# Clustered attention and two mixers on one core: a list scheduler for the order of attention, similarities in two row groups

## The chip, the cores and the metric

The kernel runs on one core of a Trainium2 chip. Its engines are TensorE (PE, matmuls; its weight loads are PEld), VectorE (DVE), ScalarE (ACT), GpSimd (POOL) and SyncE (SP, which here only issues DMAs). Each engine works through its own queue in order and waits on semaphores for the others. The metric is the device time in microseconds (us) of one execution.

## What is computed

The inputs `q`, `k`, `v` have 2 batches, 8 heads, 768 positions and 64 columns; there are 16 centroids per head.

```python
# attention: a query sees only keys of its own cluster
q_assign = argmax(einsum('bhsd,hcd->bhsc', normed(q), normed(centroids)))
k_assign = argmax(einsum('bhsd,hcd->bhsc', normed(k), normed(centroids)))
scores = where(q_assign[..., None] == k_assign[..., None, :], q @ k.T / 8, -1e9)
attn = exp(scores - max(scores)); attn = attn / (sum(attn) + 1e-9)
x = attn @ v                                    # -> [2, 768, 512]
# first mixer
x_prev = x shifted by one position
xk = mu_k * x + (1 - mu_k) * x_prev;  xr = mu_r * x + (1 - mu_r) * x_prev
x = sigmoid(xr @ w_r) * (relu(xk @ w_k) ** 2 @ w_v)
# second mixer
u = x + (relu(x.T @ w_tok1) @ w_tok2).T
return u + relu(u @ w_ch1) @ w_ch2
```

## The kernel before

**Two parts.** Attention comes first. The second part, called dense here, holds the gate of batch 1, the feed-forward and the second mixer. The gate of batch 0 (`gate_step`, `r<-wu,xmix` in the trace) begins inside the first part. Weights of the dense part arrive as 64-bit words and are turned into two fp32 halves by "splitting" a unit of 128 x 1024: `w_split`, seven instructions on VectorE and ScalarE, the last on GpSimd for the units of `w_r`. `NEARLY` units have room during attention and `NLATE` more later.

**Attention.** Two heads form a pair; there are 8 pairs, numbered 0 to 7. A pair has 12 tasks (2 halves of the queries x 3 tiles x 2 heads). For each task `score` runs four matmuls of 384 columns (`s<-ka,qa`, `s<-kb,qb`), `rowmax` takes the negative maximum on VectorE (`junk<-s`), `expo` the exponential and its row sum on ScalarE (`e<-s,nm`). The exponentials of the first half of the queries are transposed on TensorE (`transp_p`, `t<-ident,e`) and evacuated by `evac_p` (`ptp<-t`); those of the second half on VectorE (`transp_d`, `tb<-e`) and moved by 16 DMAs (`shuffle`, `ptd<-tb`). Then `pv` runs six steps per half (`x<-ptp,v`, `x<-ptd,v`, four records a step) in the PSUM bank "x"; `recip`, `rbcast` and `rbevac` make the reciprocal row sums (`ss`, `rs`, `rw`, `rb`), and `xevac` multiplies by them into `xT`.

**Preparation of the next pair.** `prep_steps(n)` prepares pair n during pair n - 1. `hi` rounds queries and keys into `qa`, `ka`, `kb` (ScalarE), `lo` subtracts for the remainders (GpSimd; VectorE in the first pair). The mask comes from cluster assignments, in two halves of the sequence: `sims` multiplies centroids and raw tiles, `sime` copies the result (`sm`), `simt` transposes it (`simsT`), then `amx`, `aeq`, `am2`, `aoh` on VectorE with `ark` on GpSimd between them find the first maximum and write a one-hot tile `oh`; `mask` transposes it (`ohT`), `mske` evacuates it and `mdma` moves it into rows 64 to 79 of `qb` and `kb`. The PSUM pool `pair` has two banks, "m" and "x". Raw tiles `t0` to `t3` hold one pair's queries and keys; `loads(n + 2)` refills them.

**What sets the order.** The program is emitted in one order, and each engine gets its instructions in it. During attention the order is a sorted list, `plan`: every operation has a position in units of tasks, `NTASK * n` plus a number from the table `WHEN` (or `EDGE` for the first and the last two pairs) plus the task's index. `WSTEP`, `WTAIL`, `MIX`, `MIX1` and `GATE` place the weight units, the mixes of the first mixer and the gate. In the dense part a small planner (`Chain`, `pump`, `spend`) keeps modelled times of the engines in `now` and puts vector work between matmuls.

**The first pair.** `prep_steps(0)` can't hide. It emits `hi` and `sims` for both heads and both halves, then both chains up to `oh`, then the masks of head 0 (`mask_first`, evacuated straight into `qb` and `kb`); head 1's `hi`, `lo` and masks follow at the positions `FIRST`. `loads(1)`, `load_v(1)` and the loads of `mu` are issued right after `prep_steps(0)`, ahead of `plan`.

Of the kernel before, what the change touches and what calls it, by code (L numbers as in the profile page):

```python
# [35 lines left out]
NEARLY = 4  # L36
NLATE = 10
TINY = 2.0**-15 * 1.125
NTASK = 2 * NT
WARM2 = 4  # L40
FIRST = [-0.515, -0.504, -0.404, 0.296, 1.323, 0.949, 1.827]
WARM = 20
LAT = 0.15
WINDOW = 0.25
RAW_US = 4.5
MOVE_US = 5.0
MM384 = 0.1735
MM512 = 0.2265
WSTEP = [28.426, 42.045, 56.144, 65.233]
GATE = [14.405, 0.231]  # L50
GSTEPS = 18
MIX1 = [15.246, 17.838, 16.995]
WGAPS = [5.52, 3.134, 4.199]
WISSUE = 12.42
WTAIL = [76.413, 67.268]
MIX = [7.577, 7.342, 11.886, 13.313]
MGAPS = [1.329, 1.452]
EDGE = {-1: {'mx': 0.114,
      'ex': 1.464,
      'my': 0.943,  # L60
      'ey': 1.009,
      'td': 2.127,
      'tp0': 2.588,
      'tp1': 3.704,
      'ev0': 2.647,
      'ev1': 4.186,
      'sh': 14.303,
      'shs': 0.028,
      'pvp': 11.505,
      'ksp': 0.139,  # L70
      'ksd': 0.297,
      'rcp': 7.733,
      'rbp': 10.443,
      'rep': 12.729,
      'xep': 15.256,
      'rcd': 14.731,
      'rbd': 16.063,
      'red': 17.933,
      'xed': 22.243,
      'pvd': 19.135},  # L80
 -2: {'pvd': 20.05,
      'ksd': 0.5,
      'xed': 22.95,
      'rbd': 17.361,
      'red': 18.893,
      'rcd': 12.291,
      'sh': 16.696,
      'shs': 0.003,
      'pvp': 11.217,
      'ksp': 0.517,  # L90
      'xep': 15.087},
 0: {'mx': 0.175,
     'ex': 1.264,
     'my': 0.055,
     'ey': 0.891,
     'td': 1.776,
     'tp0': 2.253,
     'tp1': 2.076,
     'ev0': 2.603,
     'ev1': 2.279,  # L100
     'sims0': 2.107,
     'sime0': 2.808,
     'simt0': 3.159,
     'amx0': 3.501,
     'aeq0': 3.754,
     'ark0': 4.224,
     'am20': 4.691,
     'aoh0': 4.761,
     'mask0': 6.08,
     'mske0': 6.625,  # L110
     'sims1': 4.521,
     'sime1': 5.025,
     'simt1': 5.235,
     'amx1': 5.334,
     'aeq1': 5.766,
     'ark1': 6.027,
     'am21': 6.126,
     'aoh1': 6.908,
     'mask1': 7.173,
     'mske1': 7.742,  # L120
     'mdma': 9.735,
     'hi00': 6.047,
     'hi01': 3.52,
     'hi02': 6.882,
     'hi10': 1.973,
# [105 lines left out]
def cluster_attention_moe_mixer(ctx: ExitStack, tc, q, k, v, cent, mu_k, mu_r, w_k, w_v, w_r, w1, w2, wc1, wc2, out):  # L231
# [696 lines left out]
    for e in now:  # L928
        now[e] = 0.0
# [351 lines left out]
```

## Time and profile before

| what | value |
|---|---|
| median of 3 runs | 657.71 us (656.89 to 657.90) |
| the profiled execution, its own time | 657.24 us |
| its span, first to last instruction | 655.5 us |
| TensorE busy | 626.6 us, 96% of the span |
| VectorE busy | 502.3 us, 77% |
| ScalarE busy | 371.5 us, 57% |
| GpSimd busy | 115.2 us, 18% |
| mean granted clock of TensorE | 0.994 |

The span is the profiled execution from its first to its last instruction; 1.74 us of the execution's time lie outside it. Busy shares are averages over stages with different limits: a stage has to be read by itself. A matmul's end is modelled and overlaps with the next one's start, so a busy TensorE can still hold short waits.

### The profile page before, as it was taken

To read this page: it belongs to the slowest core of one execution; us is meant where nothing else is said; L and a number is where in the kernel's file an instruction comes from. 1 tells how busy PE (TensorE), PEld (TensorE's weight loads), DVE (VectorE), ACT (ScalarE), POOL (GpSimd) and SP (SyncE) were. 2 spreads that over 40 slices of the span, in tenths; PEclk is the share of its full clock that TensorE was granted. 3 is DMA by queue.
4 is the path that set the end of the run, shared out by engine and by line. 5 is a ranking of instruction groups with operands and counts; after the bars stand their busy time and mean duration, and the time that the engine had idled before them with its cause. 6 is when DMAs were issued, how large, how long until landed. Compare 5 with 4: busy or idle time off the path is not lost.

```text
span 655.5 us, 9499 instructions
## 1 busy us (share of the span) xinstructions
PE 626.6 (96%) x3339; PEld 497.2 (76%) x3339; DVE 502.3 (77%) x900; ACT 371.5 (57%) x708; POOL 115.2 (18%) x150
## 2 busy tenths in 40 slices
PE   7889999999898999999999999999999999999997
PEld 5546556464655647789999999888999999999996
DVE  5889898988989894889985988987999733785113
ACT  4768788777787884796685666513443421332110
POOL 3235242444425238100000000010002000000000
PEclk9979999999999999999999999999999999999999
DMA  5234729475564616424430444224545412320002
GB/s 170 73 115 140 223 68 270 136 201 166 144 207 115 162 41 176 161 91 134 129 97 0 128 129 126 69 64 97 155 135 135 122 65 97 96 65 1 0 1 96
DMA packets 36735, 75.43 MB, mean 115 GB/s; under 512 B 6032, under 2 KB 19344, under 8 KB 36688
## 3 DMA queue, kind: packets, MB, share of 16 engines
q1 hardware_dynamic: 34256, 67.36, 33.7%
q0 software_dynamic: 2432, 7.47, 4.6%
q8 instruction: 26, 0.43, 0.3%
q14 instruction: 21, 0.17, 0.1%
HBM read 48.27 MB, written 3.15 MB: 78 GB/s over the span
## 4 chain that ended last, share of the span: by engine, by line
PE 80%; DVE 11%; ACT 3%; issue 3%; DMA 2%; SPq 0%; DVEq 0%; POOL 0%; ACTq 0%
PE h L1027 25%; PE acc L1051 25%; PE x L791 8%; PE s L707 8%; DVE junk L715 5%; PE r L513 4%; PE tok L1107 2%; PE tok L1190 2%; ACT e L724 2%; PE sims L590 2%; PE t L775 2%; DMA t<-k_dram 1%; DVE ptp L534 1%; DVE ss L731 1%; PE rb L741 1%
## 5 line engine op out<-in xcount | busy, mean ns | idle before, releaser
L1051 PE MATMUL acc<-wu,hl 128*128 128x512 f32 x720 | 170.5, 391 | 0.0
L1051 PEld LDWEIGHTS acc<-wu,hl 128*128 128x128 f32 x720 | 134.6, 188 | 26.7
L1027 PE MATMUL h<-ut,wu 128*128 128x384 f32 x576 | 104.4, 336 | 0.8 <-ACT ut L1160 0.7
L715 DVE TENSOR_SCALAR_CACHE_REDUCE junk<-s 128x768 bf16<-128x768 f32 x96 | 90.2, 940 | 17.9 <-PE s L707 17.5
L1027 PEld LDWEIGHTS h<-ut,wu 128*128 128x128 f32 x576 | 100.9, 188 | 3.3 <-ACT ut L1160 1.1
L724 ACT ACTIVATE e<-s,nm 128x768 f32<-128x768 f32 x96 | 86.4, 900 | 22.8 <-DVE junk L715 21.7
L1006 ACT ACTIVATE hl<-h 128x384 fp32r<-128x384 f32 x48 | 23.3, 489 | 97.2 <-PE h L1027 97.2
L1008 DVE SCALAR_TENSOR_TENSOR hl<-h,hl 128x384 fp32r<-128x384 f32 x48 | 26.6, 556 | 62.7 <-ACT hl L1006 62.2
L1027 PE MATMUL h<-xmix,wu 128*128 128x384 f32 x384 | 69.6, 336 | 0.4 <-DVE xmix L470 0.4
L406 ACT ACTIVATE wu<-g 128x512 fp32r<-128x512 f32 x62 | 39.1, 630 | 53.2 <-DVE g L402 53.2
L1027 PEld LDWEIGHTS h<-xmix,wu 128*128 128x128 f32 x384 | 67.2, 188 | 1.9 <-DVE xmix L470 0.7
L707 PE MATMUL s<-ka,qa 128*128 128x384 f32 x192 | 59.6, 392 | 3.5 <-ACT e L724 3.5
L707 PEld LDWEIGHTS s<-ka,qa 128*128 128x128 f32 x192 | 29.3, 192 | 39.4 <-ACT e L724 15.0
L707 PE MATMUL s<-kb,qb 80*128 80x384 f32 x192 | 50.5, 344 | 0.0
L1149 POOL DMA_DIRECT2D uperm<-ublk x16 | 7.9, 499 | 230.7 <-ACT h L1094 171.6
L754 DVE STREAM_TRANSPOSE tb<-e 128x768 f32<-128x768 f32 x48 | 46.3, 964 | 0.2 <-ACT e L724 0.2
L402 DVE SCALAR_TENSOR_TENSOR g<-wu,g 128x512 f32<-128x512 f32 x62 | 42.7, 689 | 3.6
L390 DVE SCALAR_TENSOR_TENSOR g<-wraw,g 128x512 uint32<-128x512 uint32 x62 | 44.3, 714 | 1.3
L775 PE MATMUL t<-ident,e 128*128 128x128 f32 x288 | 42.9, 276 | 1.7 <-DVE ptp L534 0.9
L408 DVE TENSOR_TENSOR wu<-g,wu 128x512 fp32r<-128x512 f32 x58 | 40.0, 689 | 5.4 <-ACT wu L406 3.6
L396 DVE SCALAR_TENSOR_TENSOR g<-wraw,g 128x512 uint32<-128x512 uint32 x62 | 42.4, 684 | 0.1
L394 ACT ACTIVATE wu<-wraw 128x512 fp32r<-128x512 f32 x62 | 40.6, 661 | 0.0
(103 smaller groups left out, 903.1 us busy)
## 6 DMA issues: line engine op xcount, KB each, us to landing
wraw<-moe_w_ch_dram SPq DMA_DIRECT2D x34, 512.0 KB, 3.5
ptd<-tb SPq DMA_DIRECT2D x88, 144.0 KB, 3.8
t<-q_dram SPq DMA_DIRECT2D x16, 384.0 KB, 3.8
t<-k_dram SPq DMA_DIRECT2D x16, 384.0 KB, 3.9
ptd<-tb POOLq DMA_DIRECT2D x40, 144.0 KB, 4.3
wraw<-moe_w_k_dram SPq DMA_DIRECT2D x9, 512.0 KB, 3.3
wraw<-moe_w_v_dram SPq DMA_DIRECT2D x9, 512.0 KB, 4.1
v<-v_dram SPq DMA_DIRECT2D x8, 384.0 KB, 4.1
```

The source lines that it names most:

```text
L390: nc.vector.scalar_tensor_tensor(out=g, in0=high, scalar=0xC0000000, in1=g, op0=ALU.bitwise_and, op1=ALU.bitwise_or)
L394: nc.scalar.activation(t[:, 1, :], f32(high), AF.Abs)
L396: nc.vector.scalar_tensor_tensor(out=g, in0=low, scalar=29, in1=g, op0=ALU.logical_shift_right, op1=ALU.bitwise_or)
L402: nc.vector.scalar_tensor_tensor(out=gf, in0=f32(t[:, 1, :]), scalar=TINY, in1=gf, op0=ALU.is_ge, op1=ALU.mult)
L707: nc.tensor.matmul(ps[:, nh, 0:HS], x[:, e, c0 : c0 + P], y[:, e, nh * HS : (nh + 1) * HS], start=first, stop=not first,)
L715: nc.vector.tensor_scalar(junk, PS_[t][:, :, 0:HS], -SCALE, None, op0=ALU.mult, op1=ALU.min, accum_out=nm)
L724: nc.scalar.activation(et.rearrange("p (a b) -> p a b", a=2), PS_.pop(t)[:, :, 0:HS], AF.Exp, bias=NM_.pop(t), scale=SCALE, accum_out=ss_[ ...
L754: nc.vector.transpose(out=T_[n][:, :, e, :, i, :].rearrange("p j k q -> p k j q"), in_=E_.pop(t).rearrange("p (k j c) -> p k j c", j=4, c=32),
L775: nc.tensor.transpose(ps[:, kk], E_[t][:, kt * P : (kt + 1) * P], ident)
L791: nc.tensor.matmul(o, vts[n][:, e, kt, :], m, start=(kt == 0), stop=(kt == NT - 1))
L1027: nc.tensor.matmul(ps[:, 0:HS], u[:, wl, c, :], xin(xl, c, sl), start=(n == 0), stop=(n == 11))
L1051: nc.tensor.matmul(accs[st], prev[:, xl, st * P : (st + 1) * P], u[:, wl, :], start=(idx == 1 and n == 0), stop=(idx == nf and n == 2),)
```

## The change

- **Order.** The tables of positions go. Every operation of attention becomes an `Op` with its engine, a modelled duration, a due time and the operations that it depends on; `run_plan` is a list scheduler that keeps each engine's modelled time and again and again issues the ready operation that starts first, weighed with its due time. It models a cost for switching TensorE between PV and other work, and that GpSimd and some VectorE operations exclude each other. An evacuation in `evac_p` goes to VectorE or ScalarE as the scheduler finds.
- **Similarities.** `sims` runs once per pair. The centroids `cn` fill all 128 rows (twice the same 64); the half `hf` of the sequence uses rows 64 hf to 64 hf + 63 and the bank "m" or "x".
- **Assignment.** `eq` and `rk` are written into the unused columns of `simsT` in PSUM; `ark` is on VectorE. The row sums' addition of 1e-9 and the spreading of the reciprocals (`spread`, `rw`) move to GpSimd, as does `hi(e, 2)`; `rw` gets its own tile.
- **First pair.** Head 0 goes through the whole chain by itself, with both halves in one tile (`sims_head`, `simt_head`, `aoh_head`); head 1's chain is planned among the tasks. `loads(1)`, `load_v(1)` and `mu` become planned operations.
- **Weights and tail.** `NEARLY` is 5 and `NLATE` 9. The sigmoid's table is loaded by a one-column sigmoid after the last exponential. The dense planner starts with the engines' modelled times that attention leaves.

```diff
-NEARLY = 4
-NLATE = 10
+NEARLY = 5
+NLATE = 9
...
- 'hi2': 'A',
+ 'hi2': 'P',
...
- 'rw': 'A',
+ 'rw': 'P',
...
-            def sims(hf, pool=pair, tag="m"):
-                ps = pool.tile([P, HS], F32, tag=tag, name="sims")
+            def sims():
+                for hf in range(2):
+                    st["ps", hf] = pair.tile([P, HS], F32, tag="mx"[hf], name="sims")
                 for e in range(2):
                     for j, r in ((0, qr), (1, kr)):
                         o = 32 * (2 * e + j)
-                        nc.tensor.matmul(
-                            ps[o : o + 32, :], cn[:, 2 * p + e, :], r[e][:, hf * HS : (hf + 1) * HS],
+                        for hf in range(2):
+                            rows = slice(D * hf, D * hf + D)
+                            nc.tensor.matmul(
+                                st["ps", hf][o : o + 32, :], cn[rows, 2 * p + e, :],
+                                r[e][rows, hf * HS : (hf + 1) * HS], start=True, stop=True,
+                            )
...
+            def sims_head(e):
+                st["ps", e] = ps = pair.tile([P, HS], F32, tag="m", name="sims")
+                for hf in range(2):
+                    for j, r in ((0, qr), (1, kr)):
+                        o = 32 * (2 * hf + j)
                         nc.tensor.matmul(
+                            ps[o : o + 32, :], cn[0:D, 2 * p + e, :], r[e][0:D, hf * HS : (hf + 1) * HS],
...
-                st["sv", hf] = ps.rearrange("p a b c -> p (a b) c")[:, :, 0:NC]
+                groups = ps.rearrange("p a b c -> p (a b) c")
+                st["sv", hf], st["eq", hf] = groups[:, :, 0:NC], groups[:, :, NC:]
...
             def ark(hf):
-                st["rk", hf] = rk = sml.tile([P, HT * 4, NC], F32, tag="rk", name="rk")
-                nc.gpsimd.tensor_tensor(
-                    out=rk, in0=st["eq", hf], in1=rank.unsqueeze(1).to_broadcast([P, HT * 4, NC]), op=ALU.mult
+                st["rk", hf] = rk = st["eq", hf]
+                nc.vector.tensor_tensor(
+                    out=rk, in0=rk, in1=rank.unsqueeze(1).to_broadcast([P, HT * 4, NC]), op=ALU.mult
                 )
...
+        def denom(n, hf):
+            nc.gpsimd.tensor_scalar(ss_[n, hf], ss_[n, hf], 1e-9, None, op0=ALU.add)
+
...
+        def run_plan():
+            ready, last, moved = [o for o in plan if not o.left], "", 0.0
+
+            def start(o, e):
+                t = now[e]
+                for d in o.deps:
+                    if d.e != e or e != "P":
+                        t = max(t, d.end + (0.0 if d.e == e else CROSS))
+                if e == "P":
+                    return t + (SWITCH if (o.kind == "V") != (last == "V") else 0.0)
+                if e == "G" and not o.kb:
+                    return max(t, lock[0])
+                return max(t, lock[1]) if o.two else t
+
+            while ready:
+                picks = []
+                for e in now:
+                    mine = [(start(o, e), o, e) for o in ready if e in o.e]
+                    if mine:
+                        picks.append(min(mine, key=lambda x: (x[0] + DUE_W * x[1].due, x[1].seq)))
+                t, o, e = min(picks, key=lambda x: (x[0], x[1].seq))
+                ready.remove(o)
...
+        sm = Op("P", 0.65, want(0, "f5"), first[7], tail=0.2, kind="M")
...
+        load_[1] = [Op("S", 2.0, want(0, "loads") - 9, lambda: loads(1), before, kb=1536)]
...
+                score_[g] = Op("P", 0.7, want(n, "s", j), lambda t=t: score(t),
+                               parts[n][e] + [mask_dma.get(n), exp_.get(g - 2), score_.get(g - 1)], tail=0.2)
...
+        Op("A", 1.4, want(NP - 1, "g"), lambda: nc.scalar.activation(csq[:, 0:1], half, AF.Sigmoid), [exp_[NTASK * NP - 1]])
```

## Rows read from the trace of the kernel before

**Rows 1.** Busy time by stretch: length, then each engine, clock, DMA share, GB/s
```profile
14.22:44.85 30.63, 24.88 (x142) 16.48 (x140) 26.20 (x50) 23.63 (x47) 10.19 (x7) 0.89 0.30 91
44.85:128.18 83.33, 79.72 (x496) 49.73 (x494) 75.37 (x152) 65.66 (x132) 32.97 (x33) 1.00 0.53 155
128.18:216.65 88.47, 81.35 (x500) 49.95 (x498) 80.93 (x161) 67.83 (x136) 35.93 (x36) 1.00 0.59 171
216.65:245.14 28.49, 27.02 (x157) 16.54 (x155) 25.00 (x48) 24.96 (x52) 7.78 (x9) 1.00 0.39 105
245.14:284.29 39.15, 37.89 (x173) 28.82 (x172) 27.08 (x34) 25.25 (x37) 15.86 (x12) 1.00 0.51 155
284.29:655.50 371.21, 365.83 (x1825) 329.07 (x1823) 260.85 (x443) 158.37 (x298) 7.86 (x16) 1.00 0.29 88
```

**Rows 2.** TensorE in order of time, pair 2: start, length, instructions, idle before
```profile
72.95 1.51 PE L791 MATMUL x<-ptp,v 128*64 128x384 f32 x8
...
76.10 0.85 PE L590 MATMUL sims<-t,cn 128*32 128x384 f32 x8
76.88 0.87 PE L791 MATMUL x<-ptp,v 128*64 128x384 f32 x4
...
91.43 0.34 PE L638 MATMUL ohT<-identb,oh 128*128 128x128 bf16 x3 [0.93 <-DVE oh L630]
...
93.39 0.62 PE L707 MATMUL s<-ka,qa 128*128 128x384 f32 x2 [0.18 <-ACT e L724]
```

**Rows 3.** The same view for VectorE and GpSimd, from 87 to 92 us
```profile
88.22 1.07 DVE L731 TENSOR_SCALAR ss<-ss 128x6 f32<-128x6 f32 x1
...
89.44 1.94 DVE L630 TENSOR_TENSOR oh<-rk,m 128x192 bf16<-128x192 f32 x1
...
87.46 1.80 POOL L583 TENSOR_TENSOR ka<-t,ka 64x768 fp32r<-64x768 f32 x1
89.34 3.71 POOL L583 TENSOR_TENSOR qb<-t,qa 64x768 fp32r<-64x768 f32 x2
```

**Rows 4.** Instruction groups from 44.85 to 128.18 us: busy us, mean ns, idle before
```profile
L583 POOL TENSOR_TENSOR ka<-t,ka 64x768 fp32r<-64x768 f32 x6 | 10.9, 1815 | 16.6 <-ACT ka L536 16.3
...
L630 DVE TENSOR_TENSOR oh<-rk,m 128x192 bf16<-128x192 f32 x6 | 6.9, 1148 | 0.1
...
L536 ACT ACTIVATE kb<-t 64x768 fp32r<-64x768 f32 x6 | 5.0, 835 | 0.0
...
L731 DVE TENSOR_SCALAR ss<-ss 128x6 f32<-128x6 f32 x6 | 3.7, 622 | 0.0
L621 POOL TENSOR_TENSOR rk<-eq,rank 128x192 f32<-128x192 f32 x6 | 3.6, 598 | 23.4 <-DVE eq L615 23.4
...
L615 DVE TENSOR_TENSOR eq<-simsT,mx 128x192 f32<-128x192 f32 x6 | 2.1, 351 | 0.1
```

**Rows 5.** VectorE, then TensorE in order of time, pair 6
```profile
208.07 2.21 DVE L390 SCALAR_TENSOR_TENSOR g<-wraw,g 128x512 uint32<-128x512 uint32 x1
...
212.29 0.62 PE L707 MATMUL s<-ka,qa 128*128 128x384 f32 x2 [1.25 <-ACT e L724]
```

**Rows 6.** DMA issues of the page: count, KB each, median us to landing
```profile
t<-k_dram SPq DMA_DIRECT2D x16, 384.0 KB, 3.9
```

**Rows 7.** All engines in order of time, before the first score
```profile
5.63 0.84 ACT L536 ACTIVATE ka<-t 128x768 fp32r<-128x768 f32 x1
...
6.21 0.84 PE L590 MATMUL sims<-t,cn 128*32 128x384 f32 x4 [0.42 <-POOL xT L269]
...
7.50 0.95 DVE L583 TENSOR_TENSOR qb<-t,qa 64x768 fp32r<-64x768 f32 x1
8.30 0.16 PEld L590 LDWEIGHTS sims<-t,cn 128*32 128x32 f32 x8 [0.85 <-DMA t<-k_dram]
```

**Rows 8.** Busy time by stretch around the fall of the granted clock
```profile
27.00:36.06 9.06, 6.77 (x51) 5.24 (x51) 8.99 (x20) 7.10 (x17) 6.33 (x5) 1.00 0.00 1
36.06:42.88 6.82, 5.88 (x17) 3.75 (x18) 6.15 (x11) 5.75 (x12) 1.81 (x1) 0.50 0.45 117
```

**Rows 9.** TensorE in order of time, gate of batch 1
```profile
267.66 0.73 PE L513 MATMUL r<-wu,xmix 128*128 128x512 f32 x2 [1.26 <-ACT sg L979]
```

More of the change, by code (lines that the diff above doesn't have):

```diff
@@ new lines @@
+T_FIRST = 11.753
+CROSS = 0.115
+LAND = 1.815
+SWITCH = 0.12
+DUE_W = 0.29
+DUE = {'s': 0.075,
+ 'mx': -0.216,
+ 'ex': 0.934,
+ 'td': 1.972,
+ 'tp0': 2.127,
+ 'tp1': 1.924,
+ 'ev0': 2.789,
+ 'ev1': 2.471,
+ 'sime0': 2.677,
+ 'simt0': 3.916,
+ 'amx0': 3.315,
+ 'aeq0': 4.2,
+ 'ark0': 1.675,
+ 'am20': 5.655,
+ 'aoh0': 5.342,
+ 'mask0': 6.23,
+ 'mske0': 7.093,
+ 'sime1': 5.3,
+ 'simt1': 4.15,
+ 'amx1': 7.462,
+ 'aeq1': 4.24,
+ 'ark1': 3.439,
+ 'am21': 3.014,
+ 'aoh1': 5.1,
+ 'mask1': 7.092,
+ 'mske1': 5.991,
+ 'mdma': 12.339,
+ 'hi00': 4.779,
+ 'hi01': 3.762,
+ 'hi02': 1.798,
+ 'hi10': -3.51,
+ 'hi11': 7.134,
+ 'hi12': 9.268,
+ 'lo00': 5.499,
+ 'lo01': 7.416,
+ 'lo10': 8.186,
+ 'lo11': 13.714,
+ 'loads': 11.239,
+ 'loadv': 22.628,
+ 'rcp': 8.425,
+ 'rbp': 9.723,
+ 'rep': 12.293,
+ 'rcd': 12.334,
+ 'rbd': 13.853,
+ 'red': 15.74,
+ 'pvd': 20.865,
+ 'pvp': 12.779,
+ 'xed': 21.885,
+ 'xep': 13.005,
+ 'ksp': 0.271,
+ 'ksd': 0.542,
+ 'sh': 15.329,
+ 'sims': 3.038,
+ 'f0': -1.84,
+ 'f1': 1.446,
+ 'f2': 0.203,
+ 'f3': 0.652,
+ 'f4': 0.826,
+ 'f5': -0.235,
+ 'f6': -2.65,
+ 'f7': -0.306,
+ 'f8': 0.224,
+ 'f9': 0.443,
+ 'w': 3.255,
+ 'x0': 2.468,
+ 'w2': 13.0,
+ 'x1': 10.147,
+ 'xs': 2.308,
+ 'g': 16.907}
@@ L484, in queue @@
             for c in range(KD):
-                later.append((lambda: not any(ch.done is False for ch in last[-1:]), lambda c=c: last.append(self.start(c, t + c))))
+                later.append((lambda: all(ch.done for ch in last[:-1]), lambda c=c: last.append(self.start(c, t + c))))
         def __call__(self, part, c, sl):
@@ L599, in sime, with simt @@
                 st["sm", hf] = sm
[L601 to L602 removed]
+            def simt(hf):
+                ps = pair.tile([P, HT, 4, 32], F32, tag="mx"[hf], name="simsT")
                 for i in range(HT):
@@ new lines, in run_plan @@
+        def run_plan():
[18 more added lines that the diff above has]
+                ready.remove(o)
+                if len(o.e) > 1:
+                    o.e = e
+                    o.fn(e)
+                else:
+                    o.fn()
+                now[o.e] = t + o.us
+                o.end = t + o.us + o.tail
+                if o.kb:
+                    moved = max(moved, t + 1.0) + o.kb / (235.0 if o.kb == 144 else 380.0)
+                    o.end = moved + LAND
+                elif o.e == "G":
+                    lock[1] = now["G"]
+                elif o.two:
+                    lock[0] = now[o.e]
+                if o.e == "P":
+                    last = o.kind
+                for u in o.users:
+                    u.left -= 1
+                    if not u.left:
+                        ready.append(u)
+            assert all(o.end is not None for o in plan)
```

542 lines of the change are left out of this document (279 added, 263 removed).

## The prediction

> **What bounds the kernel now.** I read the busy time by stretch first, then TensorE's and VectorE's instructions in order of time, then the durations by group. The stretches [rows 1] are cut at the first score matmul of a head pair. From 284.29 us on, TensorE is busy 365.83 of 371.21 us: that is the dense part, which the diff hardly touches. The room is before it. A pair in the regular stretch (pairs 1 to 3, 83.33 us) takes 27.8 us, with TensorE busy 79.72 of the 83.33, VectorE 75.37 and ScalarE 65.66. So TensorE is nearly the bound, and what it loses is 3.6 us in three pairs. Pairs 4 to 6, where weight units are split beside attention, take 29.5 us each and lose 7.1 us. Pair 0 takes 30.63 us with TensorE busy 24.88, part of it at half clock.
>
> The loss has one visible cause [rows 2]: in every regular pair TensorE waits 0.93 us before the transposes `ohT` and then 0.18 us for an exponential, and nowhere else for long. The releaser is VectorE's `oh<-rk,m`. VectorE's queue at that place [rows 3] shows that this instruction took 1.94 us and the tiny `ss` before it 1.07 us, each ending together with a GpSimd subtraction (87.46 + 1.80 = 89.26 and the next one). The same forms without such a neighbour are short: `eq`, of the same 192 elements, takes 351 ns on average [rows 4]. So VectorE stands still for about 2.3 us per pair, the row maxima queue behind it, the exponential is late, and TensorE ends up idle.
>
> **The change part by part. Similarities.** `sims` is issued once instead of twice per pair. Before, two calls of eight records take 0.78 us each (76.10 to 76.88) [rows 2], over 128 rows of which the lower 64 hold zeros. After, one half of the sequence lies on rows 0 to 63 and bank "m", the other on rows 64 to 127 and bank "x", as many records as one call twice over 64 rows. If the two row groups run together, a pair costs 0.78 us instead of 1.56; if they take turns, nothing is saved. The trace shows only column groups side by side (eight records of 0.5 us in 0.78 us), not row groups, so the saving is 0 to 0.78 us per pair. I take 0.78, since the column groups of the same call overlap; six pairs in the regular and weight stretches give 4.7 us. The Trainium skill's page "TensorE: Matmul & The Clock Gate" (Part 3: Packing small matmuls) says that matmuls on different row groups run at the same time, which would give the 0.78. The page "TensorEngine Tiling (Array Packing)" (Restrictions and Gotchas, PSUM Pressure) says against it that row tiles cannot use one PSUM bank together; here each has its own bank, so the sum would stay; no run here shows either yet.
>
> **The assignment chain on VectorE.** `eq` and `rk` now live in the PSUM bank of `simsT`, so `oh` has only one SBUF input; `rk` comes from GpSimd to VectorE; the `ss` addition goes to GpSimd. Per pair: `oh` 2 x (1.148 - 0.35) = 1.6 us less, `ss` 2 x 0.62 = 1.2 less, `rk` 2 x 0.35 more, taken like `eq` (351 ns) [rows 4]: 2.1 us less of VectorE's 25.1 (75.37 / 3). The bound from the other side: if `oh` in PSUM still waits for GpSimd, 0.5 us less. What the trace shows as a stall behind GpSimd's subtraction the Trainium skill states as a rule ("SBUF — State Buffer", Who interferes with whom): a VectorE instruction with two SBUF inputs and a GpSimd instruction that reads SBUF exclude each other for the whole instruction. This trace agrees, 1.94 us against 0.35.
>
> **Work moved to GpSimd.** `hi2` (two per pair, 0.835 us on ScalarE), the spreading of the reciprocals (`rw`) and the `ss` addition. No row has a GpSimd copy. The bounds for `hi2` are ScalarE's 0.8 and GpSimd's two-input form of the same shape, 1.81 us [rows 4]; I take 0.9, one input being nearer to the copy. `rw` has half the columns of `hi2`: 0.4 to 0.9. `ss` is at most the 0.6 us of `rk`. GpSimd's 11.0 us per pair (32.97 / 3) become 12.7 to 16.4 of 26, so it isn't the bound, but the row sums now pass GpSimd twice behind subtractions of 1.8 us, 2 to 4 us later. That hides behind the second half's tasks, as `xT` needs them only after six PV steps; uncovered it would cost TensorE up to 2 us per pair. ScalarE loses about 2.5 us per pair.
>
> **The order.** The list scheduler replaces hand-placed positions by an order in which every engine's queue is followed. It can't shorten the floor; it can remove the waits. It puts `oh` and `ss` where they no longer block, may put an evacuation of `transp_p` on either VectorE or ScalarE, and the weight split where GpSimd is free. In the old order a split instruction stood 2.21 us on VectorE and TensorE then idled 1.25 us [rows 5]. I leave 0.4 us of idle time in a regular pair and 0.8 us in one with a weight unit. The SP and GpSimd queues move too: `loads(1)`, `load_v(1)` and `mu` become planned operations behind the last reader of head 1's raw tiles, and SP issues in order, so the next pair's shuffles and mask DMAs stand behind them; a shuffle late by one load (3.9 us from issue to landing [rows 6]) has the gate steps or the next pair's scores as its cover, so I price it at nothing, and at 1 to 2 us once if the cover fails. The fifth weight unit adds four VectorE instructions of 0.7 us to the last stretch, where VectorE is busy 27.08 of 39.15 us [rows 1]: nothing; without that cover 2.5 us. As the same unit is then not split in the dense part, which TensorE fills, it brings nothing there either.
>
> Sum for pairs 1 to 3: 79.72 - 3 x 0.78 + 3 x 0.4 + 0.5 (a weight unit moves into pair 3) = 79.1, against 83.33: -4.2 us (bounds -5.9 and -1.5). Pairs 4 to 6: 81.35 - 2.34 + 2.4 = 81.4, against 88.47: -7.1 (bounds -9.4 and -2.5). Pair 7 has no `sims`; 27.02 busy and 0.7 idle against 28.49: -0.8 (-1.5 to +0.5).
>
> **The first pair.** Now [rows 7] the first score waits for the similarities of both heads (the last key tile lets them start at 8.30) and for both assignment chains. By head, the chain needs only the first two tiles, which have landed when `ka` starts at 5.63. From there: the first similarities some 0.3 us later than today's 6.21 because of one more VectorE instruction, then `sims_head` 0.8, copy 0.5, transposes 0.5, five VectorE instructions 1.75 behind the two `lo` (0.95 each, the second ends at 8.45), transposes 1.0, evacuations 1.1, warm-up transposes 0.6: first score at 11.8 instead of 14.22, -2.4 (-3.0 to -1.5). In the pair itself VectorE gets the chain of head 1 (1.75 us) but loses the stalls: 26.20 busy - 2.1 - 0.9 (one `lo` of 1.9 that waited for GpSimd) + 1.75 = 25.0 us, with some 2.4 us of filling and of late loads: 27.4 against 30.63, -3.2 (-6 to 0).
>
> That last range holds the clock. TensorE ran at the lower of its two levels (1.2 instead of 2.4 GHz, granted 0.50) from 36.06 to 42.88 us, after a stretch in which it was busy 6.77 of 9.06 us [rows 8]; in 6.82 us it did the work of 3.4. The new start has fewer matmuls before the first score, about 2.6 us in 5.4, so a fall may come earlier; I leave one fall of that size in the 27.4 us. Gone, it gives 3.4 us more; a second costs 3.4.
>
> **The tail.** The gate of batch 1 waits 1.26 us for the first sigmoid [rows 9], the first of its function; the change loads the table after the last exponential: -1.2 (-1.3 to 0).
>
> In all -2.4 - 3.2 - 4.2 - 7.1 - 0.8 - 1.2 = -18.9 us. The span of 655.5 becomes 636.6; with the 1.74 us outside it (657.24 - 655.5) that is 638.3, and the median of the runs lies 0.5 above the profiled one: **638.8 us**.
>
> **The rivals.** (1) *Bank "x" becomes the bound, slower than before.* The new `sims` claims both "m" and "x", and `eq` and `rk` stay in them until `oh` of both halves is read. PV accumulates in "x" and can't run meanwhile. Per pair PV needs twelve steps, 6 x 1.51 = 9.1 us [rows 2], so with a hold of h the pair takes at least 9.1 + h. Today the first half goes from `sims` at 76.10 to the other half's last `oh` at 91.38 in 15.3 us, with idle room between its parts [rows 2, 3]; 24.4 us is under 26.2, but not by much. It decides from a hold of 17 us and makes the kernel slower from 20.8: then a pair takes 29.9, which over six pairs eats the 7.6 us won at start and end. At 22 us: 31.1, six of them +14.8, less 7.6: 665. For it speaks that VectorE works in order, its ten chain instructions behind row maxima of 0.94 us; against it that the two halves now start together, so the hold should be under those 15 us. (2) *The row groups take turns*: +4.7, 643.5. (3) *GpSimd's larger load stops the weight split.* By the rows a split instruction can stand 2.2 us behind a GpSimd one; with 2 to 5 us more of GpSimd work per pair, pairs 3 to 6 keep today's loss, +5 us, 644. The page "SBUF — State Buffer" of the Trainium skill would have it so for the split's instructions with two SBUF inputs. (4) *PV is cut into single steps*: two steps together take 1.51 us, one alone 0.87 [rows 2]; each pair of steps cut apart costs 0.23, four more per pair +0.9, in eight pairs 646. (5) *The new order leaves nearly no waits and the clock doesn't fall*: 631. (6) *The change doesn't do what it says*: the waits only move, and the order is worth nothing beside the shorter `sims` and the start: 655.5 - 4.7 - 2.4 - 1.2 = 647 and 649 for the median.
>
> **How the numbers follow.** Forecast (633 to 643) 0.49; rival 1 0.09; rivals 2, 3 and 4 0.08 each; rival 5 0.08; rival 6 0.08; 0.02 no difference. The range takes in the bounds of the terms: all at their gain end -27 (630), all at their loss end -5 (652): 630 to 652 leaves out rival 1, half of the waits beyond rival 6 and a little of rival 5, below 2 in 10. 0.2%, about 1.3 us, is what a measurement of this kernel can tell: faster 0.89, the same 0.02, slower 0.09.
>
> **What would show it.** In the changed profile: `sims` in one group of 0.8 us per pair; `oh` at 0.35 to 0.4 us throughout; regular pairs of 26.2 us and weight pairs of 27.1 us from first score to first score; a first score near 11.8 us; no wait for the first sigmoid. The forecast is wrong where TensorE's idle time per pair stays at 1 us or more, above all before PV (then rival 1), where `sims` takes 1.5 us (rival 2), or where the granted clock falls more than once.

## The result, and the profile after

The changed kernel takes **636.59 us** (median of four runs, 636.45 to 638.65) against 657.81 us before: a ratio of 0.967, with a 95% interval of 0.964 to 0.969. The profiled execution is the longest of the four, 638.65 us with a span of 636.9; the other three lie between 636.45 and 636.68.

Busy time by stretch of the kernel after, cut at the same events as [rows 1] (the columns are those of that group: length, then TensorE, its weight loads, VectorE, ScalarE and GpSimd with their counts, granted clock, DMA share, GB/s):

```profile
14.29:43.79 29.50, 26.41 (x142) 19.43 (x138) 24.30 (x52) 21.19 (x43) 10.57 (x9) 0.75 0.34 112
43.79:121.45 77.66, 74.91 (x493) 50.30 (x491) 71.06 (x149) 63.90 (x132) 41.51 (x47) 1.00 0.63 176
121.45:200.97 79.52, 76.86 (x500) 50.79 (x499) 70.94 (x152) 64.81 (x133) 41.26 (x47) 1.00 0.62 174
200.97:229.56 28.59, 28.40 (x163) 16.77 (x162) 27.56 (x50) 23.88 (x46) 13.34 (x15) 1.00 0.38 98
229.56:267.01 37.45, 37.45 (x174) 28.98 (x172) 23.80 (x30) 21.02 (x32) 8.97 (x9) 1.00 0.45 134
267.01:636.90 369.89, 365.42 (x1825) 329.17 (x1823) 259.84 (x442) 157.86 (x297) 7.85 (x16) 1.00 0.28 89
```

Read against [rows 1], the 18.6 us of span went from these places:

| stretch | before | forecast | after |
|---|---|---|---|
| up to the first score | 14.22 | 11.8 | 14.29 |
| pair 0 | 30.63 | 27.4 | 29.50 |
| pairs 1 to 3 | 83.33 | 79.1 | 77.66 |
| pairs 4 to 6 | 88.47 | 81.4 | 79.52 |
| pair 7 | 28.49 | 27.7 | 28.59 |
| gate | 39.15 | 37.95 | 37.45 |
| dense part | 371.21 | 371.2 | 369.89 |

The total is the forecast one, but not its parts: the six pairs in the middle gave 14.6 us instead of 11.3, the first 44 us gave 1.1 instead of 5.6. The rest of this text asks why.

TensorE of the kernel after in order of time, in pair 1 (start, length, instructions, idle before and its releaser), the place that answers to [rows 2]:

```profile
46.39 2.16 PE L818 MATMUL x<-ptp,v 128*64 128x384 f32 x12
...
52.00 0.88 PE L581 MATMUL sims<-t,cn 64*32 64x384 f32 x16 [0.20 <-ACT rb L524]
52.81 0.62 PE L729 MATMUL s<-ka,qa 128*128 128x384 f32 x2
...
56.61 0.55 PE L621 MATMUL simsT<-ident,sm 128*128 128x128 f32 x3 [0.48 <-ACT sm L615]
...
60.86 0.34 PE L655 MATMUL ohT<-identb,oh 128*128 128x128 bf16 x3
...
61.53 2.16 PE L818 MATMUL x<-ptd,v 128*64 128x384 f32 x12 [0.33 <-issue]
```

Three things are to be seen. The sixteen similarity records of a pair take 0.81 us from their start to the next score (52.00 to 52.81), where eight took 0.78 us before [rows 2]. The 0.93 us of idle time before `ohT` is gone; the small waits that are left are for `rb`, ScalarE's evacuation of the spread reciprocals (0.20), for a copy of the similarities (0.48) and single issues. And PV products now run twelve records at a time, in 2.16 us, where before they ran eight (1.51) and four (0.87).

Instruction groups of the kernel after from 43.79 to 121.45 us (busy us, mean ns, idle before), to be set beside [rows 4]:

```profile
L571 POOL TENSOR_TENSOR qb<-t,qa 64x768 fp32r<-64x768 f32 x6 | 10.9, 1823 | 1.1 <-ACT qa L524 0.9
...
L526 POOL CAST kb<-t 64x768 fp32r<-64x768 f32 x6 | 5.3, 887 | 0.1
...
L526 POOL COPY rw<-rs 128x384 f32<-128x384 f32 x6 | 3.0, 503 | 4.1 <-DVE rs L756 4.0
...
L647 DVE TENSOR_TENSOR oh<-simsT,m 128x192 bf16<-128x192 f32 x6 | 2.1, 357 | 0.2
L752 POOL TENSOR_SCALAR ss<-ss 128x6 f32<-128x6 f32 x6 | 1.4, 232 | 25.1 <-ACT e L746 25.1
```

`oh` costs 357 ns each time instead of 1148 on average, and the moved pieces have their prices on GpSimd: 887, 503 and 232 ns.

The start went otherwise. TensorE of the kernel after, up to the first score (compare [rows 7]):

```profile
6.15 0.85 PE L591 MATMUL sims<-t,cn 64*32 64x384 f32 x8 [0.43 <-issue]
...
10.42 1.46 PE L675 MATMUL ohT<-identb,oh 128*32 128x128 bf16 x12 [2.25 <-DVE oh L606]
...
12.85 1.50 PE L591 MATMUL sims<-t,cn 64*32 64x384 f32 x8
14.29 1.01 PE L729 MATMUL s<-ka,qa 128*128 128x384 f32 x2
```

The chain of head 0 is there early, as planned: similarities at 6.15, `oh` ready by 10.42. But the similarities of head 1 (12.85) stand ahead of the first score, and the same eight records that took 0.85 us at 6.15 take 1.50 us at 12.85. The stretches of the same kernel around the granted clock say why (columns as above):

```profile
5.61:8.61 3.00, 1.50 (x13) 0.49 (x11) 2.51 (x4) 1.16 (x2) 1.10 (x2) 1.00 1.03 347
8.61:14.29 5.68, 3.87 (x25) 2.11 (x25) 2.56 (x6) 1.81 (x3) 1.35 (x2) 0.50 0.93 329
14.29:22.27 7.98, 7.82 (x37) 6.44 (x33) 5.77 (x12) 3.84 (x7) 1.74 (x2) 0.50 0.40 133
...
35.92:42.75 6.83, 6.15 (x19) 4.40 (x19) 6.00 (x10) 4.02 (x9) 1.48 (x2) 0.50 0.67 203
```

Up to 5.61 TensorE runs the 20 `warm` transposes that open both kernels. From there to 8.61 it was busy 1.50 us of 3.00, and from 8.61 to 22.27 it ran at the lower level (1.2 GHz, granted 0.50), then again from 35.92 to 42.75. The kernel before had the second of these falls alone [rows 8].

### The profile page after: what moved, and what is told of

It reads as the page before. It is cut to its first block, busy times and chain, and to the rows that moved or that the text cites. A ratio compares the mean times of both kernels' runs of the same rounds, so it can differ in the third digit from the quotient of the medians.

```text
span 636.9 us, 9517 instructions
## 1 busy us (share of the span) xinstructions
PE 619.1 (97%) x3339; PEld 502.2 (79%) x3339; DVE 484.3 (76%) x889; ACT 358.3 (56%) x689; POOL 129.3 (20%) x181
## 4 chain that ended last, share of the span: by engine, by line
PE 82%; DVE 6%; ACT 6%; issue 2%; DMA 1%; POOL 1%; SPq 0%; DVEq 0%; ACTq 0%
PE h L1199 26%; PE acc L1223 25%; PE x L818 9%; PE s L729 8%; PE r L501 5%; ACT e L746 3%; DVE junk L737 3%; PE tok L1279 2%; PE t L802 2%; PE tok L1362 1%; ACT ptp L524 1%; PE sims L581 1%; PE rb L768 1%; DMA uperm<-ublk 1%; DVE x L1375 1%
## 5 line engine op out<-in xcount | busy, mean ns | idle before, releaser
L737 DVE TENSOR_SCALAR_CACHE_REDUCE junk<-s 128x768 bf16<-128x768 f32 x96 | 90.3, 941 | 16.4 <-PE s L729 14.7
```

Source lines behind the costliest of these rows:

```text
L737: nc.vector.tensor_scalar(junk, PS_[t][:, :, 0:HS], -SCALE, None, op0=ALU.mult, op1=ALU.min, accum_out=nm)
```

## The experiments

Ratios are to the kernel before, each in the same set of runs, with 95% intervals; "the kernel after" is the changed one. The kernel before had medians of 657.8 to 660.7 us in the four sets of runs, so times from different sets can differ by 2 or 3 us without a cause in the kernel; stretches of the profiles tell more there. Five questions were open: what the start costs, what the two row groups are worth, what keeps `oh` short, what the fifth weight unit does, and what of the gain is the order.

### The start and the clock

The kernel after again, unchanged, and then with identity transposes put where TensorE waits in the start:

```diff
                 sime(0)
+                keep_warm(4)
                 simt_head(0)
...
+                keep_warm(18)
                 mask_first(0, 0, "m"), mask_first(1, 0, "x")
...
+        def keep_warm(count):
+            for _ in range(count):
+                nc.tensor.transpose(warm[:, 0], ident, ident)
```

> The changed kernel once more, beside the others on the same chip. Theory: the profiled execution (638.65 us, clock at half for 20.5 us around the first pair) is a slow-start one; the other three (636.5 us, mean clock 0.992 to 0.995, so 6 to 10 us at half) are the usual case, so the median is 636.5. In a usual execution the first score should come before 13.3 us instead of 14.3. Rival: the late start is in every execution and the 2 us come from somewhere else.

> The changed kernel with 22 idle transposes of the identity put into TensorE's waits before the first score (4 before the transposes of the similarities, 18 while VectorE does head 0's assignment). Theory A: the clock fell at 8.6 us because TensorE had little to do there, and that fall put the first score at 14.3 us instead of 11.8; with the transposes the clock stays up, the first score comes at 12.3 to 13 and the kernel gains 1.5 to 3 us on the profiled execution (and up to 1 us on the median). Rival B: the first pair is bound by VectorE and ScalarE, so an earlier first score is given back before pair 1 and the time stays within 0.5 us.

The unchanged kernel gave 637.74 us, 0.967 (0.962 to 0.971). Its profile has the late start once more: first score at 14.66, half clock from 9.80 to 23.45 and from 37.1 to 40.5. The mean granted clock of its four executions is 0.985 to 0.986. So the late start belongs to the kernel and not to one profile, against the theory; but it isn't in every execution, as three of the four in the first set have a mean clock of 0.992 to 0.995 and are 2 us faster than the profiled one (0.984).

With the transposes: 635.47 us, 0.963 (0.959 to 0.967), 2.3 us less than the kernel after in the same set of runs. That makes it the best of all versions here. Its stretches to the end of pair 3, and TensorE in its start:

```profile
0.00:13.04 13.04, 10.70 (x79) 8.43 (x79) 6.74 (x18) 5.51 (x9) 5.16 (x39) 1.00 0.80 272
13.04:39.47 26.43, 20.32 (x143) 14.67 (x139) 23.56 (x52) 21.12 (x43) 12.19 (x9) 1.00 0.35 116
39.47:117.23 77.76, 74.98 (x493) 50.31 (x491) 71.64 (x149) 64.06 (x132) 41.48 (x47) 1.00 0.65 185
```

```profile
8.18 2.13 PE L835 MATMUL warm<-ident 128*128 128x128 f32 x18
10.59 0.84 PE L675 MATMUL ohT<-identb,oh 128*32 128x128 bf16 x12 [0.28 <-DVE oh L606]
...
12.26 0.85 PE L591 MATMUL sims<-t,cn 64*32 64x384 f32 x8 [0.24 <-DVE qb L681]
13.04 0.62 PE L732 MATMUL s<-ka,qa 128*128 128x384 f32 x2
```

The granted clock is 1.00 wherever the profile records it, from 5.55 us on; `ohT` takes 0.84 us instead of 1.46 and the second similarities 0.85 instead of 1.50. The first score comes 1.25 us earlier and pair 0 is 3.1 us shorter than in the profile after (1.6 and 1.9 against the repeated one); pairs 1 to 3 are the same within 0.1 us. So the half clock in the start is shown to cost some 2 to 4 us. The other profiles bear it out: in the eight of versions with these transposes the recorded clock doesn't fall before 26 us, in the four without them it falls at 8.6 to 10.4 us. What the transposes don't do is raise it earlier: in one of the eight (four weight units) the first record of full clock stands at 10.52 us, the similarities at 6.52 take 1.51 us, and the first score comes at 14.52; in the other seven it comes at 13.0 to 13.5. The half clock does not explain all of the miss: with a full clock the first score still comes at 13.04 and not 11.8; head 1's similarities (12.26 to 13.04) are ahead of it.

The Trainium skill speaks against this fix: "TensorE: Matmul & The Clock Gate" (Part 4: PE-mode transpose) says that a transpose doesn't count as TensorE being busy in the way a matmul does, so 22 transposes shouldn't hold the clock. Here they did (1.00 against 0.50 from 8.61 on), and the measurement decides. The trace lists them as MATMUL; whether they ran in the mode that the page means, no run here shows.

### The two row groups

The similarities over 128 rows with zeros in the lower half, one half of the sequence after the other, as they were before, all else unchanged:

```diff
-                for e in range(2):
-                    for j, r in ((0, qr), (1, kr)):
-                        for hf in range(2):
-                            rows = slice(D * hf, D * hf + D)
+                for hf in range(2):
+                    for e in range(2):
+                        for j, r in ((0, qr), (1, kr)):
...
-                                st["ps", hf][o : o + 32, :], cn[rows, 2 * p + e, :],
-                                r[e][rows, hf * HS : (hf + 1) * HS], start=True, stop=True,
+                                st["ps", hf][o : o + 32, :], cn[:, 2 * p + e, :],
+                                r[e][:, hf * HS : (hf + 1) * HS], start=True, stop=True,
...
-        nc.vector.tensor_copy(cn[:, :, 0:NC], pc.rearrange("p (h c) -> p h c", h=H))
+        nc.vector.tensor_copy(cn[0:D, :, 0:NC], pc[0:D].rearrange("p (h c) -> p h c", h=H))
```

> The changed kernel with similarities as before: 128 rows, the lower 64 of the centroids zero, the two halves one after the other, all else and the order the same. Theory: sims takes 1.5 us per pair instead of 0.81 (2.43 us in three pairs), TensorE is the bound, so 7 pairs cost 7 x 0.76 = 5.3 us more: 641.9. Rival: TensorE's idle 0.9 us per pair takes it up, then less than 2 us.

It gave 641.20 us, 0.972 (0.967 to 0.976), 3.5 us more than the kernel after in the same set. Pairs 1 to 3 and 4 to 6 of this version, and TensorE in its pair 1:

```profile
43.67:123.17 79.50, 76.79 (x493) 51.02 (x491) 71.21 (x149) 64.29 (x132) 41.56 (x47) 1.00 0.64 177
123.17:204.60 81.43, 78.75 (x500) 51.50 (x498) 70.99 (x152) 65.19 (x133) 41.32 (x47) 1.00 0.61 171
```

```profile
51.89 1.50 PE L580 MATMUL sims<-t,cn 128*32 128x384 f32 x16 [0.20 <-ACT rb L524]
53.31 0.62 PE L728 MATMUL s<-ka,qa 128*128 128x384 f32 x2
```

Each is 1.9 us longer than its row after, all of it TensorE busy time: 0.62 us per pair. The sixteen records take 1.43 us in this form (start to next start) and 0.81 in the other, with every engine's instructions in the same order. Fewer rows alone don't explain it: in the first pair eight records of 64 rows on one row group take 0.85 us (6.15), as eight of 128 rows do [rows 2]. So the row groups run beside each other, and rival 2 falls. "TensorE: Matmul & The Clock Gate" of the Trainium skill (Part 3: Packing small matmuls) says this of row groups, and the trace agrees. The loss is less than was expected of this run because the sixteen records of this form, issued in one go, take 1.43 us and not twice 0.78.

### What keeps `oh` short

The kernel with the warm start, and `rk` put back into SBUF (as bf16), so that `oh` has two SBUF inputs again:

```diff
-                st["rk", hf] = rk = st["eq", hf]
+                st["rk", hf] = rk = sml.tile([P, HT * 4, NC], BF16, tag="rk", bufs=1, name="rk")
                 nc.vector.tensor_tensor(
-                    out=rk, in0=rk, in1=rank.unsqueeze(1).to_broadcast([P, HT * 4, NC]), op=ALU.mult
+                    out=rk, in0=st["eq", hf], in1=rank.unsqueeze(1).to_broadcast([P, HT * 4, NC]), op=ALU.mult
```

> On top of warm_start (clock full throughout, so its stretches can be compared to 0.1 us): the ranked candidates are written to SBUF again (as bf16, 1 to 16 exactly), so oh has two SBUF inputs as before the change; the order is the same. Theory: oh stands behind GpSimd's instruction wherever one runs; GpSimd is busy 53% of a pair with instructions of 1.8 us, so the 14 oh average 0.9 us instead of 0.36, some of 1.5 to 2 us, the pairs lose 0.5 us or more each: 3 to 8 us, 638 to 643. Rival: the list scheduler's order keeps oh out of GpSimd's way, or the idle time takes it up: under 1 us.

It gave 636.32 us, 0.965 (0.963 to 0.968): not to be told from the warm start's 0.963. VectorE's `oh` and its GpSimd neighbours in order of time, pair 0 and the first of pair 1:

```profile
29.33 0.87 DVE L647 TENSOR_TENSOR oh<-rk,m 128x192 bf16<-128x192 bf16 x1
32.64 0.67 DVE L647 TENSOR_TENSOR oh<-rk,m 128x192 bf16<-128x192 bf16 x1
54.84 0.36 DVE L647 TENSOR_TENSOR oh<-rk,m 128x192 bf16<-128x192 bf16 x1
```

```profile
28.18 1.81 POOL L571 TENSOR_TENSOR ka<-t,ka 64x768 fp32r<-64x768 f32 x1
...
32.28 0.82 POOL L526 CAST kb<-t 64x768 fp32r<-64x768 f32 x1
```

In pair 0 `oh` stands twice behind a GpSimd instruction (0.87 us beside the subtraction that ends at 29.99, 0.67 beside the copy). Of the twelve `oh` after it eleven take 0.36 us, as in the row of pair 1, and one takes 0.42. With the warm start alone, the first of pair 0 meets the same subtraction, VectorE and GpSimd:

```profile
28.54 0.36 DVE L647 TENSOR_TENSOR oh<-simsT,m 128x192 bf16<-128x192 f32 x1
```

```profile
27.38 1.82 POOL L571 TENSOR_TENSOR ka<-t,ka 64x768 fp32r<-64x768 f32 x1
```

With one SBUF input it takes 0.36 us while the subtraction runs. So the exclusion that the prediction cited is real, and the move into PSUM does avoid it; but it matters only where the two meet. Pair 0 and pairs 1 to 3 of the version with two SBUF inputs:

```profile
13.22:41.08 27.86, 20.31 (x142) 14.68 (x138) 24.99 (x52) 21.11 (x43) 11.56 (x9) 1.00 0.33 109
41.08:118.77 77.69, 74.95 (x492) 50.30 (x490) 71.59 (x149) 63.96 (x132) 41.50 (x47) 1.00 0.65 184
```

Pair 0 is 1.4 us longer than the warm start's 26.43, of which the two `oh` are 0.8 and a subtraction of VectorE that meets GpSimd by another timing is 0.6. Pairs 1 to 3 (77.69 against 77.76) and 4 to 6 (79.5 against 79.55) lose nothing: there the order already keeps `oh` clear of GpSimd, and the move into PSUM, to which I gave the saving, is worth nothing measurable.

The same question from the other side: the kernel before, with two GpSimd subtractions given a later place by hand.

```diff
- 'lo00': 6.934,
- 'lo01': 6.742,
+ 'lo00': 7.734,
+ 'lo01': 7.542,
```

> The kernel before with one thing moved: GpSimd's two subtractions of head 0 of the next pair (lo00, lo01 in WHEN) stand 0.8 tasks later, so that oh of the second half doesn't meet them. Theory: oh takes 0.36 instead of 1.94 us in pairs 1 to 6, TensorE's wait of 0.93 + 0.18 us there goes, 6 x 1.1 = 6.6 us less: ratio 0.990. Rival: the wait only moves to the next instruction with two SBUF inputs or to the exponential, ratio 0.997 to 1.003.

It gave 658.15 us, 0.999 (0.996 to 1.001). VectorE, then GpSimd, in pair 2 of this version:

```profile
89.80 1.93 DVE L630 TENSOR_TENSOR oh<-rk,m 128x192 bf16<-128x192 f32 x1
```

```profile
87.81 1.82 POOL L583 TENSOR_TENSOR ka<-t,ka 64x768 fp32r<-64x768 f32 x1
```

The stall of `oh` is still there, instruction for instruction as in [rows 3]. GpSimd's queue differs from that of the kernel before in one place only, where a weight subtraction moved ahead of `ka`, and the other queues are the same: the later place put nothing new in front of the subtractions in their own queue here, and they start with the same neighbours as before. My theory (-6.6 us) fell, but the run didn't take the stall away, so it says nothing about the stall's worth. It does show that a later place in the program's order need not delay anything: what counts is what stands ahead in the same engine's queue.

### The fifth weight unit

Four units beside attention as before, ten later; without and with the warm start:

```diff
-NEARLY = 5
-NLATE = 9
+NEARLY = 4
+NLATE = 10
```

> The changed kernel with 4 early weight units and 10 late ones, as before the change. Theory: the fifth unit is hidden on both sides, so the time stays within 0.7 us. Rival: the 1.3 us that the dense part won came from it; then 637.8 and the dense part from its first matmul is 371.2 us again instead of 369.9.

> On top of warm_start: 4 early weight units and 10 late ones. In four_units the dense part waited 2.0 us for weights of the first feed-forward and took 372.6 instead of 369.9 us, but its clock also was at half for 27 us. Theory: the unit is worth 2 to 3 us by itself, at full clock too: 637.5 to 638.5, with TensorE waiting for wu at the first feed-forward. Rival: it was the clock; then 635.5.

The first gave 642.79 us, 0.974 (0.968 to 0.979), the second 638.64, 0.969 (0.966 to 0.973) against 0.963 with five units. What TensorE waited for in the dense part of the second (sum, times, longest):

```profile
PE h L1206 <- DVE wu L396: 1.5, 2, 1.2
PE h L1206 <- ACT wu L394: 0.6, 1, 0.6
```

These 2.1 us are waits for split weights at the first feed-forward, which the kernel after doesn't have. The dense part takes 372.93 us (372.6 without the warm start) against 369.85: the unit is worth 3 us here. The first version lost 5 us to the kernel after in the same set of runs; the rest lies ahead of its dense part, and its profile has the half clock for 27.3 us against 17.1 in that of the unchanged kernel. Why it fell for longer is not shown. The kernel before had four units and no such wait: it had time to split more before its dense part. Of the step `wu<-g` on ScalarE 56 were left to the dense part in the kernel before and in the kernel after, 57 in the two versions with four units (counted in the traces). With 14 and 20 us less ahead of the dense part in these two, the split is what comes late next.

### What of the gain is the order

Four versions of the kernel with the warm start. First the weight of the due times set to nothing, so that the list scheduler picks by its own start times alone:

```diff
-DUE_W = 0.29
+DUE_W = 0.0
```

> On top of warm_start: the weight of the due times is 0, so the list scheduler takes what can start first. Theory: the list scheduler alone doesn't give the gain; without the due times it runs ahead with whatever is ready, starves what the next pair needs, and the time is at least 10 us above warm_start, as in warm_no_switch_cost. Rival: the due times only polish: within 3 us.

It gave 741.21 us, 1.124 (1.119 to 1.128). TensorE's longest waits by releaser (sum, times, longest), and the stretch of its pairs 1 to 3:

```profile
PE s L732 <- ACT e L749: 19.5, 21, 2.2
PE ohT L655 <- DVE oh L647: 17.0, 6, 4.1
PE t L805 <- ACT e L749: 12.1, 15, 1.9
```

```profile
58.17:170.25 112.08, 87.17 (x475) 58.22 (x474) 76.62 (x157) 59.02 (x120) 31.69 (x37) 0.82 0.39 110
```

Pairs 1 to 3 take 112.08 us against 77.76. With the same instructions, the same engines and the same row groups, a bare list order is 12% slower than the order written by hand. The granted clock falls again and again as well (0.82 in this stretch). So the scheduler wins only together with its fitted due times.

Next its price for a change between PV and other matmuls:

```diff
-SWITCH = 0.12
+SWITCH = 0.0
```

> On top of warm_start: the scheduler is told that going from PV to other work costs TensorE nothing. Its order then has 104 changes between PV and other work instead of 84. Theory: a change costs 0.16 us (before to after, pairs 1 to 3: 46 changes became 32 while score and PV records took 2.9 us less), so 20 more cost 3.2 us: 638.7. Rival: those 2.9 us have another source; then under 1 us.

It gave 655.99 us, 0.995 (0.992 to 0.997). Its pair 4, and its wait before `ohT` over the whole span:

```profile
121.76:157.94 36.18, 31.29 (x172) 19.66 (x170) 28.98 (x56) 22.85 (x47) 16.28 (x18) 0.86 0.55 161
```

```profile
PE ohT L655 <- DVE oh L647: 7.3, 7, 1.5
```

Changes between PV and other work rise from 84 to 104 (counted in the trace over the pairs): ten more runs of PV, some 2 us at the 0.18 us per run found below. The loss is 20 us: one pair takes 36.18 us instead of some 26.5, and `ohT` waits 7.3 us instead of 1.0. So this number steers the order as a whole; its own price is the smaller part.

The same with the assumed delay between engines, 0.115 us, made 0.01 larger:

```diff
-CROSS = 0.115
+CROSS = 0.125
```

> On top of warm_start: the modelled delay between engines is 0.125 us instead of 0.115, everything else the same. Theory: the order is fitted to these very numbers, and a small change gives another order that isn't as good: 3 to 15 us more. Rival: the scheduler's order is good for any model near the chip's times: within 1.5 us.

It gave 640.80 us, 0.972 (0.968 to 0.976), 5 to 6 us worse. Its pairs 1 to 3 and 4 to 6 take 79.70 and 83.55 us, against 77.76 and 79.55. So the constants work as one fit with the due times: moving one of them by a little lost part of the good order. Whether another value with due times fitted to it would do better, no run here shows.

Last, `hi2` and the spreading `rw` back on ScalarE: once with the scheduler told of it, and once with the order of issue left as it is.

```diff
- 'hi2': 'P',
+ 'hi2': 'A',
...
- 'rw': 'P',
+ 'rw': 'A',
```

> On top of warm_start: the third rounding copy of each head and the spread of the reciprocals go back to ScalarE, and the scheduler knows it. ScalarE gets 2.7 us more per pair (21.4 to 24 of 26.4), GpSimd 2.8 less. Theory (mine): TensorE bounds a pair, so at most 0.3 us per pair, 0 to 2 us in all. Rival: ScalarE was the late engine (its exponentials release most of TensorE's waits), so the pairs become 27.4 and the time 8 us longer.

> On top of warm_start: the third rounding copy and the spread on ScalarE as in warm_hi2_on_scalar, but the scheduler isn't told, so every other instruction keeps its place. Theory: ScalarE at 23.6 of 26.4 us per pair still has room, the loss of 11 us in warm_hi2_on_scalar came from the other order; here 0 to 3 us more than warm_start. Rival: the load is the cause; then 8 us or more again.

The first (the scheduler's operations for the two are changed to ScalarE as well) gave 646.76 us, 0.982 (0.979 to 0.986); the second 638.67, 0.968 (0.965 to 0.972). Pairs 1 to 3 and 4 to 6 of the first, then of the second:

```profile
40.45:121.52 81.07, 75.34 (x491) 49.59 (x491) 71.04 (x148) 70.19 (x144) 32.57 (x34) 1.00 0.61 174
121.52:207.13 85.61, 78.70 (x501) 51.59 (x499) 73.10 (x151) 71.49 (x146) 34.78 (x36) 0.98 0.58 162
```

```profile
41.59:120.61 79.02, 75.33 (x492) 50.12 (x491) 71.37 (x149) 69.78 (x144) 33.51 (x35) 1.00 0.62 176
120.61:200.60 79.99, 77.21 (x500) 50.59 (x499) 70.92 (x152) 70.41 (x145) 33.59 (x35) 1.00 0.61 173
```

ScalarE's load is nearly the same in both (70 us of 80). The move to GpSimd is worth 1.3 + 0.4 us in the six pairs when the order is kept, and 3 us in all with pair 0, where the clock fell (half from 36.9 to 40.3). The other 8 us of the first version come with its new order, for which the due times weren't fitted.

## Why the prediction was right, and where its steps failed

**Right in the total, by misses that cancel.** 638.3 us were forecast for the profiled execution and 638.65 came, 638.8 for the median and 636.59 came. 18.9 us were forecast and 18.6 came (spans). The middle pairs gave 3.3 us more than forecast and the gate and the dense part 1.8 more; the first 44 us gave 4.6 less and pair 7 0.9 less.

**Similarities: right.** Forecast 0.78 us per pair, measured 0.76 (4.70 us before and 2.43 after in three pairs, start to next start, from the two traces). Of this the row groups are shown to carry 0.62.

**The assignment chain: size right, cause wrong in the regular pairs.** `oh` fell to 357 ns as said. VectorE's time fell by 1.4 us per pair (75.37 to 71.06 in three) where 2.1 were forecast, but the chain's own part is the forecast one: in the two traces `oh` and `ss` give 8.5 us in three pairs and `rk` takes 2.2, which is 2.1 a pair. Nine evacuations `ptp` that went to ScalarE give 4.9 more, and the split of a weight unit, which stood in later pairs before, takes 6.4. The step that failed is that the one SBUF input of `oh` makes it short: the input does so in pair 0, but in the six pairs after it the run with two SBUF inputs keeps the gain. There the order does it, by keeping GpSimd's subtractions away from `oh`.

**Work moved to GpSimd: right.** `hi2` 0.887 us (0.9 taken), `rw` 0.503 (0.4 to 0.9), `ss` 0.232 (at most 0.6), GpSimd 13.8 us per pair (12.7 to 16.4). Of the row sums one small wait of TensorE is left, the 0.2 us of `sims` for `rb` in each of the six pairs; whether the move caused it is not shown. The step on ScalarE was wrong in its net: it was to lose 2.5 us per pair, and lost 0.6 (65.66 to 63.90 in three). `hi2` and `rw` took 8.2 us away in three pairs (2.7 a pair), but nine evacuations `ptp` (4.6 us) and four steps of the weight split (2.6) came in their place.

**The order in pairs 1 to 3: a term mis-sized, another missing.** Idle time was to fall from 3.6 to 1.2 us and fell to 2.75 (77.66 - 74.91). But TensorE's busy time fell by 4.8 us, not by the 1.8 of the sum (2.34 for `sims`, less 0.5 for the added unit). The missing term is rival 4 with its sign turned: PV is not cut into single steps, but joined into runs, half of them of three. In pairs 4 to 6, 144 PV records come in 24 runs before and 16 after and take 27.05 and 25.64 us (start to next start without idle time, from the traces): 0.18 us for each run saved and 0.158 for a record. These two prices give 26.24 and 24.37 us for the PV records of pairs 1 to 3 before (140 in 23 runs) and after (136 in 16), where the traces have 26.26 and 24.34; in the orders of the other experiments, at full clock, they are up to 0.35 us short. The score matmuls between the runs take 0.7 us less too in pairs 4 to 6 (30.96 to 30.27), and 1.0 in pairs 1 to 3; why is not shown. I had the price of a run from [rows 2] (0.23) and never asked whether the scheduler would make runs longer. No run changes the length of the runs alone, so this term is read from the traces and not tested.

**Pairs 4 to 6: right in the waits.** Idle time 7.1 to 2.66 us (2.4 forecast). The 1.9 us beyond the forecast are the same missing term, 1.4 in the PV records and 0.7 in the scores, less 0.26 of idle time.

**Pair 7: a matter of the cut.** TensorE was to be busy 27.02 us and was 28.40. The stretch has eight PV records more (72 against 64): more of a pair's products now lie behind the next pair's first score, and pairs 1 to 3 have fewer (136 against 140). The 72 take 12.67 us and the 64 took 11.38, 1.3 us less. Pairs 1 to 7 together, where the cuts fall out: 188.2 us forecast, 185.8 measured.

**First score: failed.** Forecast 11.8 us, measured 14.29. Three steps failed. The terms don't add up to the 11.8: from 8.45, with 1.75, 1.0, 1.1 and 0.6 one after the other, they give 12.9, and 11.8 only if the evacuations (1.1) cost nothing. Measured with the clock held, transposes, evacuations and warm-up transposes take 1.7 us together (10.53 to 12.26). Head 1's similarities are issued before the first score (0.8 us); my chain went straight from the warm-up transposes to the score. And the clock fell at 8.61. I had named it ("a fall may come earlier") and put it into pair 0's range, but not into the first score. With the clock held, 13.04 is measured.

**Pair 0: failed in the same way.** 27.4 us forecast with one fall, 29.50 with two stretches at the lower level. With none, 26.43: so the sum without clock, which would be 24.0 (27.4 less 3.4), was 2.4 us too short as well. Of the 6.1 us that TensorE idles there, which wait is the one that counts was not settled.

**Gate: right.** No wait for the sigmoid is left; TensorE is busy 37.45 of 37.45 us. The early load of the table was not run by itself.

**Dense part: the step "it brings nothing" failed.** The cover, VectorE's free time in the gate, was there. The sum set the unit against a kernel before that had time enough for the split; shorter attention takes that time away, and without the fifth unit 2.1 us of waits appear. Of the 3 us, about 1 is not placed.

**The rivals.** Bank "x" (1): in pair 1 it is held from 52.00 to 61.53, some 9.5 us, far from the 17 at which it would decide. Row groups in turn (2): fell, by the run. The split stopped by GpSimd (3): fell, by 2.66 us of idle time in three weight pairs. Single PV steps (4): the opposite came. No waits and no fall of the clock (5): the waits went and the clock fell twice; with the clock held the ratio is 0.963, 633.5 us against the 657.8 of the kernel before, and 631 was forecast for it. Waits that only move (6, 649 us): fell; but the two runs with one constant set to nothing (656 and 741 us) are slower than that.

## What to carry to other kernels

Ask of a new order not only which waits it removes but which neighbours it joins: the waits removed are 0.9 us in pairs 1 to 3 and 4.5 in pairs 4 to 6, and longer runs of PV with the scores between them come to some 2 in each. A planner with fitted due times is one object here: changing a constant, an engine or a cost in it without fitting again cost 5 to 106 us, more than the part under test, so test a part with the order of issue held. And where a chain before the first large matmul is made shorter in TensorE's work, look at the granted clock there, and fill its waits with harmless matmuls if it falls.

## What was not expected of the hardware

- 22 more identity transposes in the waits of the start, 2.8 us of TensorE time, keep the granted clock at 1.00 from its first record (5.55 us) to the end of the profiled execution; without them it is 0.50 from 8.61 to 22.27 us and once more from 35.92 to 42.75. The two falls are not bound to each other: the kernel before and the version with `hi2` and `rw` on ScalarE in the kept order have the later one alone (36.06 and 36.9 us).
- Two row groups of 64 rows and four column groups of 32 run sixteen records in 0.81 us; one row group of 128 takes 1.43 us for the same sixteen.
- A run of PV matmuls (64-column weights) between others costs about 0.18 us beside its records, by the count of runs and times in two traces.
- A VectorE `oh` of 0.36 us with two SBUF inputs takes 0.87 us beside a GpSimd subtraction and 0.67 beside a GpSimd copy; with one of the two in PSUM it takes 0.36 us in the middle of the same subtraction.
- A GpSimd copy of 64x768 takes 0.887 us, about half of the 1.82 us of the two-input subtraction of the same shape.
